# A linear-attention and channel-mix kernel: another written-out order, with a margin between VectorE's two-operand operations and GpSimd's, and k's exponentials placed without regard to k's maximum

## The chip, the cores and the metric

The kernel runs on one core of a Trainium2 chip. Its engines work side by side, each through its own queue in program order: TensorE (PE), VectorE (DVE), ScalarE (ACT), GpSimd (POOL) and SyncE (SP, which here only issues DMAs). The metric is the device time of one launch in microseconds. The time before is the median of three runs.

## The reference, cut to what matters

Two blocks, one after the other, for 8 batches of 576 positions:

- Attention, 8 heads of 64 wide: k and q are each projected by one 64 x 128 matrix; of every projected row the largest absolute value is subtracted (P - m), and phi is the concatenation of exp and exp of the negative of the shifted row, 256 features. Then kv = phi(k)^T v, z = the column sums of phi(k), and the output is phi(q) kv / (phi(q) z + 1e-6). There is no softmax over positions.
- Channel mix on the 576 x 512 result x: each row is mixed with the row before it, xk = mu_k x + (1 - mu_k) x_prev and likewise xr; then v = relu(xk Wk)^2 Wv with 1024 inner features, r = sigmoid(xr Wr), and the output is r v in float32.

## The kernel before, in words

**Tiling.** A batch has four *pairs* of heads; 32 pairs n = 4 b + a. Of a pair's positions eight chunks of 128 lie in "ps_k" and "ps_q", two PSUM banks each; the ninth part of every head, the *edge*, is handled for a whole batch at once (tp, rt, ekt, eqe and so on). The names of the steps of a pair, with their lines:

- kp, qp (PE, L570): the projections of k and q into PSUM. rk, rq (DVE, L583 and L588): the negated largest absolute value of each row, nmk and nmq.
- ea, eb (ACT, L609): exp of +ps_k and of -ps_k, 1024 columns each, read from the same PSUM tile that rk reads. The maximum isn't subtracted here; it enters through em (ACT, L595), which writes exp of +nmk and -nmk beside v, and va, vb (POOL or DVE, L601), which multiply v by it.
- kv (PE, L660), kc (copy to SBUF): the product with v. mh, mt, mc, qt (L619 to L640): q's projection once more, transposed and with its maximum added by a matmul; qa, qb (ACT, L647): its exponentials. nd (PE, L681): numerator and denominator; ra, rd (DVE, L689 and L693): the division, giving x.
- x is transposed by PE for pairs 0 to 7 (xt, xe, xf) and by a DMA that SP issues for the others (xz at L704, then xu, a shifted copy). df (L730): the difference of two neighbouring rows, DVE or POOL, two SBUF operands. xa and xb (DVE, L736): xk and xr from it, again two SBUF operands (SCALAR_TENSOR_TENSOR).
- For a batch: h (PE, L815, eight of four matmuls each), rl (relu: ACT L206 or DVE L208), sq (square: ACT, DVE or POOL, L212 and L214), r (PE, L834) and th (ACT, L840), v (PE, L848) and ob (DVE, L854), so (SP, L861: stores). he, rle, sqe, re, the, ve, obe, soe do the same for the edge of two batches.
- lk, lq (POOL, L324) and lv (POOL or SP, L330) load k, q and v; pt (PE, L341) transposes k and q of batches 0 and 1, pa and pb copy the result to qkT; for later batches SP issues a DMA transpose (tr, L355). lv goes into "vt", three buffers.

**PSUM** has three double tiles P0 to P2 and two single ones, M0 and M1; the number behind a colon in the order says which. "+9@0" asks for nine filling matmuls (L292) ahead of an operation.

**What sets the order.** The order of all 1498 operations is written out, in the string ORDER. A name may carry the engine behind a slash. The kernel runs through the list and issues each operation on its engine's queue; the list was made elsewhere by a planner, from the durations, dependences and "port" marks that the calls of op() still name. The kernel itself doesn't read these: op() keeps the function, the buffers and the choice of engine, and drops the rest, as these lines show. The semaphore waits are put in by the Tile framework, from what the instructions read and write, in program order.

```python
def op(self, name, eng, w, at, fn, deps=(), alloc=(), rel=(), chain=None, mode=0, port=False, alt=()):
    assert name not in self.ops, name
    self.ops[name] = dict(name=name, fn=fn, alloc=alloc, alt=alt, pe=mode if eng == "PE" else None)
```

Of the kernel before, what the change touches and what calls it, by code (L numbers as in the profile page):

```python
# [19 lines left out]
ident ones hk hq dve2 hk.d hq.d wphi wphi.d lk0.1 lk0.1.d lq0.1 lq0.1.d mus mus.d lk0.2 lk0.2.d dve3  # L20
lq0.2 lq0.2.d lv0.0/POOL lv0.0.d lk0.0.d/ACT lq0.0.d/DVE pt0.0:0+9@0 pt0.1:1 pa0/ACT pb0/DVE tr0
dve1 tp0.0:0+1@2 kp0:1 rt0.0 qp0:2 rk0 ekt0.0 mhe0.0/POOL lk1.0 lk1.0.d mte0.0:0+4@1 rq0 pt1.0:0 ea0
pt1.1:1 lq1.0 lq1.0.d pa1/ACT mce0.0/DVE pb1/DVE tr1 lv0.1/POOL lv0.1.d eb0 tp0.1:0+1@4 qp1:2
lv0.2/POOL lv0.2.d rt0.1 rq1 eme0.0 kp1:1+1@1 mh0/POOL ekt0.1 qte0.0:0 mhe0.1/POOL em0 rk1 eme0.1
eqe0.0 lk1.2 lk1.2.d mte0.1:2+3@1 pt2.0:1 mce0.1/ACT mt0:0 pt2.1:0 mh1/POOL pa2/DVE ea1 pb2/DVE tr2
va0/POOL pt3.0:1+1@4 mc0/DVE qp2:2 em1 pa3/DVE mt1:0 eb1 pt3.1:0 mc1/DVE vb0/POOL rq2 qt0:0 kp2:1
qa0 lq1.2 lq1.2.d pb3/DVE tr3 kv0:2 rk2 qb0 lk2.0 lk2.0.d pt4.0:0 mh2/POOL kc0/DVE ea2 pa4/DVE
va1/POOL mt2:0+2@1 qp3:2 mc2/DVE eb2 qt1:0 rq3 wk.0 wk.0.d qte0.1:0 pt4.1:1 eqe0.1 tp0.2:1 vb1/POOL
qa1 rt0.2 pt5.0:0 nd0:2 pb4/DVE tr4 ekt0.2 mhe0.2/POOL pa5/DVE pt5.1:1 ra0 qb1 rd0 lv1.0/POOL
lv1.0.d kp3:1 rk3 wk.1 wk.1.d wk.d eme0.2 kv1:2+1@0 em2 qp4:0 wr.0 wr.0.d kc1/ACT rq4 pb5/ACT tr5  # L30
mte0.2:2+1@0 xt0:0 wr.1 wr.1.d wr.d ea3 pt6.0:1 vb2/POOL mce0.2/DVE pa6/DVE qp5:0 eb3 qt2:2 rq5
qte0.2:1 mh3/POOL qa2 kp4:1 va2/POOL xe0/DVE mt3:0 xf0/DVE em3 mc3/DVE rk4 pt6.1:0 qb2 mh4/POOL
kv2:0 df0/POOL eqe0.2 kc2/DVE nd1:2 pb6/DVE tr6 ea4 nd2:0 lq2.0 lq2.0.d ra1 rd1 pt7.0:0 eb4 va3/POOL
pt7.1:1 ra2 pa7/DVE qt3:2 pb7/ACT tr7 rd2 mt4:1 xt1:0 vb3/POOL qa3 xf1/DVE xe1/DVE tp1.0:0 mc4/DVE
qb3 rt1.0 wv.0 wv.0.d kv3:1 kc3/ACT kp5:2 xa0 ekt1.0 xt2:0 nd3:1 rk5 mhe1.0/POOL xf2/ACT eme1.0
xe2/ACT df1/POOL ra3 ea5 rd3 xb1 eb5 xt3:0+7@1 mte1.0:1 qt4:0 xa1 xf3/ACT xe3/ACT qp6:2 xb0
mce1.0/ACT qa4 qt5:1+1@1 df2/DVE tr2.0 tr2.0.d tr8 tr9 qte1.0:0 df3/DVE qb4 xa2 em4 xa3 qp7:0+3@1
qa5 vb4/POOL rq6 h0.0:1+1@1 qb5 lv1.2/SP lv1.2.d va4/POOL rq7 tr2.2 tr2.2.d tr10 tr11 kp6:2
rl0.0/ACT kp7:1 eqe1.0 vb5/POOL rk6 kv4:0 sq0.0/ACT h0.1:1 kc4/ACT mh6/POOL rk7 ea6 va5/POOL nd4:0
eb6 h0.2:0 ra4 lk3.0 lk3.0.d rd4 rl0.1/ACT kv5:2 lv2.0/SP lv2.0.d xb3 rl0.2/ACT mt6:0 h0.3:1 kc5/ACT  # L40
xb2 mc6/ACT em6 ea7 sq0.1/DVE qp8:0 vb6/POOL nd5:2 rq8 eb7 r0.0:0 va6/POOL ra5 rl0.3/ACT rd5 tp2.0:1
th0.0 qt6:0 sq0.2/POOL rt2.0 qp9:2 qa6 h0.4:0 lq3.0 lq3.0.d rq9 qb6 r0.1:1 sq0.3/POOL ekt2.0
rl0.4/DVE qp10:0 qt7:2 wv.1 wv.1.d wv.d rq10 th0.1 kp8:1 vb7/POOL qa7 h0.5:0 rk8 mhe2.0/POOL qb7
kv6:0 rl0.5/DVE xt4:1 sq0.4/POOL kc6/ACT kp9:2 ea8 nd6:0 rk9 va7/POOL h0.6:0 eb8 tr3.0 tr3.0.d tr12
tr13 ra6 mh8/POOL rd6 eme2.0 qp11:1 sq0.5/POOL rl0.6/ACT rq11 kv7:0 em8 sq0.6/ACT vb8/POOL h0.7:0
ea9 kc7/DVE xf4/DVE xe4/DVE tr3.2 tr3.2.d tr14 tr15 mt8:0 nd7:1 va8/POOL mc8/ACT rl0.7/DVE eb9 qt8:0
ra7 rd7 va9/POOL qa8 mte2.0:2 xt5:0 mce2.0/DVE kv8:1 xe5/DVE vb9/POOL qb8 qte2.0:1 kc8/DVE kp10:2
xf5/DVE eqe2.0 qt9:1 rk10 df4/POOL lv2.2/SP lv2.2.d kp11:0 r0.2:0 lv3.0/SP lv3.0.d sq0.7/ACT rk11
mh10/POOL ea10 v0.0:1 lk4.0 lk4.0.d th0.2 df5/DVE qa9 xa4 v0.1:0 ob0.0 eb10 xa5 qb9 xb5 kv9:2 em10
xb4 tp3.0:1 ea11 v0.2:1 rt3.0 vb10/POOL kc9/ACT eb11 lq4.0 lq4.0.d ob0.1 nd8:2 ekt3.0 ob0.2  # L50
va10/POOL so0.1 so0.1.d nd9:0 ra8 rd8 mt10:1 xt6:1 vb11/POOL mc10/ACT xt7:0 eme3.0 ra9 xz8 xz8.d
qt10:1 xf6/ACT xe6/ACT rd9 kv10:2 va11/POOL qa10 xe7/DVE kp12:0 xz9 xz9.d kc10/DVE r0.3:1 rk12 qb10
df6/POOL kp13:2 so0.2 so0.2.d xf7/ACT th0.3 kv11:1 rk13 df7/POOL ea12 v0.3:0 kc11/DVE eb12 xa6 xa7
em12 qp12:1 ea13 qt11:0 rq12 va12/POOL h1.0:1 tr4.0 tr4.0.d tr16 tr17 eb13 mhe3.0/POOL ob0.3 qp13:1
rl1.0/ACT nd10:2 rq13 qa11 h1.1:1 qb11 xb6 h1.2:0 ra10 xb7 rl1.1/ACT mte3.0:0 nd11:1 mce3.0/ACT
# [105 lines left out]
def kernel(  # L161
# [58 lines left out]
    op = plan.op  # L220
# [5 lines left out]
    ident = consts.tile([128, 128], BF, name="ident")  # L226
# [813 lines left out]
```

## Time and profile before

| | |
|---|---|
| median of 3 runs | 277.08 us (276.7 to 278.89) |
| profiled execution | 277.05 us, its span 275.3 us |
| PE, DVE, ACT, POOL busy | 260.7, 229.5, 223.2, 157.8 us |
| largest groups | v on POOL 62 x 1205 ns; k and q exponentials on ACT 64 x 1042 each; maxima on DVE 32 x 1217 and 32 x 1216; xk and xr on DVE 64 x 836 |
| DMA | 42.89 MB, 156 GB/s on average |

The profile names instructions by line and by the tile written and read (out<-in). Its first part gives busy time per engine; the second cuts the span into 40 slices and gives the busy share of each in tenths; stretches of any length can be asked for as a table. A line of the waits reads: engine, tile and line that stood idle, what it waited for, the total in us, how often, the longest. A line of the time line gives the start, the duration, the engine, the line, the operation, and in square brackets the idle time before it with its releaser. An engine that isn't the bottleneck may idle at no cost.

### The profile page before, as it was taken

To read this page: it belongs to the slowest core of one execution; us is meant where nothing else is said; L and a number is where in the kernel's file an instruction comes from. 1 tells how busy PE (TensorE), PEld (TensorE's weight loads), DVE (VectorE), ACT (ScalarE), POOL (GpSimd) and SP (SyncE) were. 2 spreads that over 40 slices of the span, in tenths; PEclk is the share of its full clock that TensorE was granted. 3 is DMA by queue.
4 is the path that set the end of the run, shared out by engine and by line. 5 is a ranking of instruction groups with operands and counts; after the bars stand their busy time and mean duration, and the time that the engine had idled before them with its cause. 6 is when DMAs were issued, how large, how long until landed. Compare 5 with 4: busy or idle time off the path is not lost.

```text
span 275.3 us, 8896 instructions
## 1 busy us (share of the span) xinstructions
PE 260.7 (95%) x3692; PEld 153.8 (56%) x3736; DVE 229.5 (83%) x366; ACT 223.2 (81%) x410; POOL 157.8 (57%) x218
## 2 busy tenths in 40 slices
PE   7798999999999999999999899999999999999994
PEld 2465745565755655665565466565556654444552
DVE  5899999999999999999999799888849799834222
ACT  3699999999999999989989899999997855552430
POOL 5899827995858766596648863844565205111010
PEclk9999999999999999999999999999999999999999
DMA  7999999999997897979998899775244523504044
GB/s 152 217 234 231 205 189 196 204 147 241 203 185 139 200 219 165 206 209 182 197 187 166 130 194 208 176 229 64 64 116 100 63 62 66 133 5 116 2 114 114
DMA packets 65880, 42.89 MB, mean 156 GB/s; under 512 B 47152, under 2 KB 57008, under 8 KB 65840
## 3 DMA queue, kind: packets, MB, share of 16 engines
q1 hardware_dynamic: 54544, 27.77, 48.8%
q0 software_dynamic: 10992, 14.12, 29.6%
q8 instruction: 29, 0.48, 0.7%
q10 hardware_dynamic: 304, 0.43, 0.5%
q14 instruction: 11, 0.09, 0.1%
HBM read 33.62 MB, written 9.44 MB: 156 GB/s over the span
## 4 chain that ended last, share of the span: by engine, by line
PE 76%; ACT 9%; DVE 7%; issue 2%; DMA 2%; SPq 1%; POOL 1%; DVEq 0%; ACTq 0%; POOLq 0%
PE ps_v L848 19%; PE ps_h L815 17%; PE ps_r L834 10%; PE ps_nd L681 6%; PE ps_kv L660 5%; ACT q L647 4%; PE ps_qT L634 2%; PE ps_he L903 2%; PE ps_k L570 2%; ACT k L609 2%; PE ps_qT L640 2%; PE ps_q L570 2%; DMA vt<-in_v_dram 2%; PE ps_ve L935 2%; DVE nmk L583 2%
## 5 line engine op out<-in xcount | busy, mean ns | idle before, releaser
L601 POOL TENSOR_TENSOR v<-vt,v 128x576 bf16<-128x576 f32 x62 | 73.5, 1205 | 36.2 <-ACT v L595 33.5
L609 ACT ACTIVATE k<-ps_k 128x1024 bf16<-128x1024 f32 x64 | 64.0, 1042 | 1.3 <-DVE nmk L583 1.1
L647 ACT ACTIVATE q<-ps_qT 128x1024 bf16<-128x1024 f32 x64 | 63.0, 1042 | 2.2 <-PE ps_qT L640 2.0
L815 PE MATMUL ps_h<-xk,wk_bf 128*128 128x512 bf16 x239 | 62.3, 380 | 1.1 <-issue 0.2
L848 PE MATMUL ps_v<-wv_bf,kk 128*128 128x512 bf16 x240 | 58.2, 379 | 0.8 <-issue 0.2
L730 POOL TENSOR_TENSOR diff<-xs 128x576 bf16<-128x576 bf16 x21 | 28.1, 1347 | 30.9 <-DVE xr L736 19.1
L588 DVE TENSOR_REDUCE nmq<-ps_q 128x8 f32<-128x1024 f32 x32 | 38.7, 1216 | 1.1 <-PE ps_q L570 1.0
L848 PEld LDWEIGHTS <-kk 128*128 128x128 bf16 x256 | 23.8, 98 | 27.1 <-issue 0.2
L583 DVE TENSOR_REDUCE nmk<-ps_k 128x8 f32<-128x1024 f32 x32 | 38.5, 1217 | 0.5 <-PE ps_k L570 0.2
L854 DVE SCALAR_TENSOR_TENSOR ob<-rt,ps_v 128x512 f32<-128x512 bf16 x32 | 21.7, 684 | 18.0 <-PE ps_v L848 12.9
L815 PEld LDWEIGHTS <-wk_bf 128*128 128x128 bf16 x256 | 22.7, 98 | 24.7 <-issue 0.5
L206 ACT ACTIVATE krelu<-ps_h 128x512 bf16<-128x512 f32 x40 | 23.8, 607 | 15.2 <-PE ps_h L815 15.2
L834 PE MATMUL ps_r<-wr_bf,xr 128*128 128x512 bf16 x121 | 31.9, 380 | 0.4
L840 ACT ACTIVATE rt<-ps_r 128x512 bf16<-128x512 f32 x32 | 19.4, 608 | 14.7 <-PE ps_r L834 12.2
L214 POOL TENSOR_TENSOR kk<-krelu 128x512 bf16<-128x512 bf16 x17 | 17.8, 1047 | 18.2 <-ACT krelu L206 13.8
L693 DVE TENSOR_TENSOR x_sc<-ps_nd,rden 128x640 bf16<-128x640 f32 x32 | 26.0, 818 | 0.7
L736 DVE SCALAR_TENSOR_TENSOR xk<-diff,mu_k_t,xs 128x576 bf16<-128x576 bf16 x32 | 26.3, 836 | 0.1
L736 DVE SCALAR_TENSOR_TENSOR xr<-diff,mu_r_t,xs 128x576 bf16<-128x576 bf16 x32 | 26.3, 837 | 0.0
L660 PE MATMUL ps_kv<-v,k 64*128 64x65 bf16 x1024 | 22.7, 190 | 1.6 <-DVE x_sc L693 0.7
L208 DVE TENSOR_SCALAR krelu<-ps_h 128x512 bf16<-128x512 f32 x24 | 16.4, 683 | 8.8 <-PE ps_h L815 8.0
L660 PEld LDWEIGHTS <-k 64*128 64x128 bf16 x1024 | 19.7, 94 | 6.7 <-DVE nmq L588 1.5
L212 ACT ACTIVATE kk<-krelu 128x512 bf16<-128x512 bf16 x35 | 22.1, 641 | 1.3 <-DVE krelu L208 1.2
(105 smaller groups left out, 416.9 us busy)
## 6 DMA issues: line engine op xcount, KB each, us to landing
out_dram<-ob SPq DMA_DIRECT2D x70, 128.0 KB, 2.5
vt<-in_v_dram SPq DMA_DIRECT2D x12, 576.0 KB, 4.7
nat<-in_k_dram POOLq DMA_DIRECT2D x6, 576.0 KB, 6.8
nat<-in_q_dram POOLq DMA_DIRECT2D x6, 576.0 KB, 7.9
vt<-in_v_dram POOLq DMA_DIRECT2D x3, 576.0 KB, 6.7
wk_bf<-in_moe_w_k_dram POOLq DMA_DIRECT2D x2, 512.0 KB, 8.7
wv_bf<-in_moe_w_v_dram POOLq DMA_DIRECT2D x2, 512.0 KB, 8.5
nat<-in_k_dram POOLq DMA_DIRECT2D x3, 288.0 KB, 6.3
```

The source lines that it names most:

```text
L583: nc.vector.tensor_reduce(t[:, j, :], s["k"].rearrange("p a (g f) -> p (a g) f", f=128), axis=AX.X, op=ALU.max, apply_absolute_value=True, ...
L588: nc.vector.tensor_reduce(t[:, j, :], s["q"].rearrange("p a (g f) -> p (a g) f", f=128), axis=AX.X, op=ALU.max, apply_absolute_value=True, ...
L601: (nc.vector if eng == "DVE" else nc.gpsimd).tensor_tensor(vb[:, a, pn, :, 0:64], vt[b, a // 2][:, a % 2, :].rearrange("p (s d) -> p s d", ...
L609: nc.scalar.activation(s[f"k{pn}"], s["k"].rearrange("p a (g f) -> p (a g) f", f=128), AF.Exp, scale=(1.0 if pn == 0 else -1.0))
L647: nc.scalar.activation(t.rearrange("f x (a p) -> f x a p", a=2), s["qT"].rearrange("f a (x p) -> f x a p", p=64), AF.Exp, scale=(1.0 if pn ...
L660: nc.tensor.matmul(ps[:, hh, pn * 65:(pn + 1) * 65], lhsT=s[f"k{pn}"][r, c, :], rhs=vb[r, a, pn, 2 * g + par, :], start=(pn == 0 and c == ...
L693: nc.vector.tensor_tensor(s["x"].rearrange("p (b s) d -> p b s d", b=2), s["ndv"][:, :, :, 0:64], s["rd"].to_broadcast([128, 2, 5, 64]), o ...
L730: (nc.vector if eng == "DVE" else nc.gpsimd).tensor_tensor(s["d"], xs[:, a, 64:64 + S], xs[:, a, 0:S], op=ALU.subtract)
L736: nc.vector.scalar_tensor_tensor(out=t[:, a, (b % 2) * S:(b % 2 + 1) * S], in0=s["d"], scalar=mu[:, a:a + 1], in1=xs[:, a, 0:S], op0=ALU.m ...
L815: nc.tensor.matmul(ps, lhsT=wk_bf[:, c, fc * 128:(fc + 1) * 128], rhs=xkt[bp][:, c, m0:m0 + 512], start=(c == 0), stop=(c == NDC - 1))
L834: nc.tensor.matmul(ps, lhsT=xrt[bp][:, c, m0 + ci * 128:m0 + (ci + 1) * 128], rhs=wr_bf[:, c, :], start=(c == 0), stop=(c == NDC - 1))
L848: nc.tensor.matmul(ps, lhsT=s["kk"][:, fc, ci * 128:(ci + 1) * 128], rhs=wv_bf[:, fc, :], start=(fc == 0), stop=(fc == NFC - 1))
```

## The change

The string ORDER is replaced by another arrangement of the same 1498 operations, with other choices of engine and PSUM tile. In two calls of op() a named dependence is exchanged: ekt, the edge's exponentials of k, names tp instead of rt, and ea names kp instead of rk. In the new list the steps that have a choice of engine are spread so (before, then after):

| step | before | after |
|---|---|---|
| sq, sqe | ACT 39, DVE 13, POOL 20 | ACT 30, DVE 22, POOL 20 |
| rl, rle | ACT 47, DVE 25 | ACT 44, DVE 28 |
| df | DVE 11, POOL 21 | DVE 15, POOL 17 |
| va, vb | DVE 2, POOL 62 | DVE 3, POOL 61 |
| kc | ACT 17, DVE 15 | ACT 21, DVE 11 |
| mc, mce | ACT 16, DVE 12 | ACT 11, DVE 17 |
| xe, xf | ACT 7, DVE 9 | ACT 9, DVE 7 |
| xu | ACT 9, DVE 2, POOL 13 | ACT 10, DVE 3, POOL 11 |
| pa, pb | ACT 4, DVE 12 | ACT 2, DVE 14 |
| mhe | POOL 10 | POOL 9, DVE 1 |
| lv | POOL 5, SP 12 | SP 17 |
| filling matmuls | 36 | 28 |

The diff, cut to the ends of the list, the places of ea and rk of pairs 14, 21 and 24, and the two calls:

```diff
@@ -17,115 +17,114 @@
 ORDER = """
-ident ones hk hq dve2 hk.d hq.d wphi wphi.d lk0.1 lk0.1.d lq0.1 lq0.1.d mus mus.d lk0.2 lk0.2.d dve3
-lq0.2 lq0.2.d lv0.0/POOL lv0.0.d lk0.0.d/ACT lq0.0.d/DVE pt0.0:0+9@0 pt0.1:1 pa0/ACT pb0/DVE tr0
-dve1 tp0.0:0+1@2 kp0:1 rt0.0 qp0:2 rk0 ekt0.0 mhe0.0/POOL lk1.0 lk1.0.d mte0.0:0+4@1 rq0 pt1.0:0 ea0
-pt1.1:1 lq1.0 lq1.0.d pa1/ACT mce0.0/DVE pb1/DVE tr1 lv0.1/POOL lv0.1.d eb0 tp0.1:0+1@4 qp1:2
-lv0.2/POOL lv0.2.d rt0.1 rq1 eme0.0 kp1:1+1@1 mh0/POOL ekt0.1 qte0.0:0 mhe0.1/POOL em0 rk1 eme0.1
...
-so7.0.d so6.3 so6.3.d r7.3:0 ob7.1 he3.1:0 so7.1 so7.1.d th7.3 th7.2 v7.2:0 sqe3.0/ACT rle3.1/ACT
-sqe3.1/POOL v7.3:1 ob7.2 so7.2 so7.2.d re3:0 ob7.3 ve3.0:2 so7.3 so7.3.d the3 ve3.1:1 obe3.0
-soe3.0.b soe3.0.b.d soe3.0.a soe3.0.a.d obe3.1 soe3.1.a soe3.1.a.d soe3.1.b soe3.1.b.d
+ones ident hk hq dve2 hk.d hq.d wphi wphi.d lk0.1 lk0.1.d lq0.1 lq0.1.d lv0.0/SP lv0.0.d lk0.2
+lk0.2.d dve3 mus mus.d lq0.2 lq0.2.d lk1.0 lk1.0.d lk0.0.d/ACT lq1.0 lq1.0.d lq0.0.d/DVE lv0.1/SP
+lv0.1.d pt0.0:0+9@0 lk1.2 lk1.2.d pt0.1:1 pa0/ACT lv0.2/SP lv0.2.d pb0/DVE tr0 lq1.2 lq1.2.d dve1
+lv1.0/SP lv1.0.d tp0.0:0+1@2 kp0:1 rt0.0 qp0:2 rk0 eme0.0 mhe0.0/POOL ekt0.0 pt1.0:0+1@1 pt1.1:1
+wk.0 wk.0.d mte0.0:0 pa1/DVE mce0.0/ACT pb1/ACT tr1 rq0 wk.1 wk.1.d wk.d ea0 qp1:0+1@2 qte0.0:1 rq1
+kp1:2 mh0/POOL eb0 rk1 em0 mt0:0+3@0 tp0.1:1 eqe0.0 vb0/POOL pt2.0:0 mc0/ACT ekt0.1 pt2.1:1 pa2/DVE
...
+tr18 tr19 kc12/ACT kp14:2 qte3.0:1 sq1.2/POOL rq14 qp15:0 eqe3.0 r1.0:0 sq1.1/POOL rq15 ea14 nd11:1
+xu9/POOL h1.3:1 mh12/POOL th1.0 rk14 xu8/POOL vb13/POOL mt12:0 h1.4:0 rl1.3/ACT so0.1 so0.1.d ra11
...
+kp21:1 kc19/ACT qt20:0 ob2.1 ea21 qp23:2 lv5.2/SP lv5.2.d xa14 r2.3:0 eb21 rq23 df16/POOL v2.2:1
+qa20 rk21 xu17/POOL qb20 xu18/POOL df17/POOL nd19:2 th2.3 qt21:1 ra19 ob2.2 lk7.0 lk7.0.d h3.0:0
...
+he1.0:1 sq3.7/DVE tr7.0 tr7.0.d tr28 tr29 xb19 qb22 v3.0:0 xa19 qa23 rle1.0/DVE ea24 nd22:0
...
+r3.3:0 qb23 rk24 kv23:0 th3.3 xa18 kp25:1 kc23/ACT qt24:2 eme6.0 qp27:0 rle1.1/DVE df20/POOL qa24
...
+sq7.6/POOL th7.0 so6.2 so6.2.d r7.2:1 h7.7:0 he3.0:1 rl7.7/ACT th7.2 sq7.7/DVE he3.1:0 th7.1 v7.0:1
+rle3.1/ACT rle3.0/ACT sqe3.1/POOL v7.1:0 sqe3.0/DVE ob7.0 so7.0 so7.0.d r7.3:1 ob7.1 v7.2:2 so7.1
+so7.1.d th7.3 v7.3:0 ob7.2 so7.2 so7.2.d re3:2 ob7.3 ve3.0:1 so7.3 so7.3.d the3 ve3.1:2 obe3.0
+soe3.0.b soe3.0.b.d obe3.1 soe3.1.b soe3.1.b.d soe3.1.a soe3.1.a.d soe3.0.a soe3.0.a.d
 """
@@ -530,7 +529,7 @@
            alloc=[("mTe", ("mTe", tag))])
         op(f"eme{tag}", "ACT", 0.35, ("eme", it), eme, [f"rt{tag}"], rel=[("me", tag)],
            alloc=[("v1", ("v1", b))] if first else [], chain="eme")
-        op(f"ekt{tag}", "ACT", 0.4 + 0.21 * n, ("ekt", it), ekt, [f"rt{tag}"], rel=[A])
+        op(f"ekt{tag}", "ACT", 0.4 + 0.21 * n, ("ekt", it), ekt, [f"tp{tag}"], rel=[A])
         op(f"qte{tag}", "PE", 0.1 + 0.11 * n, ("qte", it), qte, [f"mce{tag}"],
            alloc=[("mo", ("mo", "q" + tag))], rel=[("mTe", tag), ("qkT", b)], mode=1)
         op(f"eqe{tag}", "ACT", 0.4 + 0.21 * n, ("eqe", it), eqe, [f"qte{tag}"], rel=[("mo", "q" + tag)])
@@ -754,7 +753,7 @@
             op("mc" + U, "DVE", 0.22, (K("mc"), n), mc, ["mt" + U], rel=[("P", "m" + U)], alloc=[("mT", ("mT", u))],
                chain="mc", alt=("DVE", "ACT"))
             op("em" + U, "ACT", 0.35, (K("em"), n), em, both("rk") + [f"eme{pt}"], rel=[("nmk", u)])
-        op("ea" + N, "ACT", 1.03, (K("ea"), n), ek(0), ["rk" + N], alloc=al("kpn"), rel=[("P", "k" + N)],
+        op("ea" + N, "ACT", 1.03, (K("ea"), n), ek(0), ["kp" + N], alloc=al("kpn"), rel=[("P", "k" + N)],
            chain="ea")
         op("eb" + N, "ACT", 1.03, (K("eb"), n), ek(1), ["ea" + N], rel=[("P", "k" + N)])
         for pn, vn in enumerate(("va", "vb")):
```

## The prediction

> **What bounds the kernel now.** I read the page first, its 40 slices, then the busy time by stretch, then who waited for whom.
>
> ```profile
> span 275.3 us, 8896 instructions
> PE 260.7 (95%) x3692; PEld 153.8 (56%) x3736; DVE 229.5 (83%) x366; ACT 223.2 (81%) x410; POOL 157.8 (57%) x218
> PE   7798999999999999999999899999999999999994
> DVE  5899999999999999999999799888849799834222
> ACT  3699999999999999989989899999997855552430
> POOL 5899827995858766596648863844565205111010
> ```
>
> PE is full from the third slice on; DVE and ACT are full too until about slice 22 and fall off towards the end, POOL never. The stretches say how much slack each has (the columns are length, then busy time and count for PE, weight loads, DVE, ACT, POOL):
>
> ```profile
> 20.00:40.20 20.20, 17.87 (x365) 12.76 (x365) 19.96 (x37) 19.22 (x40) 13.72 (x22) 1.00 1.14 204
> 40.20:60.00 19.80, 18.66 (x343) 10.94 (x345) 19.00 (x26) 19.70 (x36) 17.63 (x23) 1.00 1.17 197
> 60.00:80.00 20.00, 19.61 (x356) 12.38 (x360) 19.33 (x32) 19.27 (x35) 15.24 (x16) 1.00 1.11 200
> 80.00:112.50 32.50, 32.11 (x520) 19.93 (x523) 31.42 (x44) 30.57 (x56) 22.20 (x38) 1.00 0.94 184
> 139.00:169.50 30.50, 29.45 (x453) 17.79 (x454) 27.34 (x40) 28.69 (x54) 18.49 (x27) 1.00 0.90 172
> ```
>
> Three stages follow. Up to 40.2 us DVE leads (0.24 us idle in 20.2): ps_h can start only after the last xk of batch 0, which ends at 40.23; PE starts its first ps_h weight load at 40.25. From 40 to about 140, PE, DVE and ACT all run at 94 to 99%. After that PE alone is full. PE idles 14.6 us in all: 2.0 before 7.2, 4.5 up to 40.2, 1.5 up to 80, about 2.9 from there to its end at 271.6, and the last 3.7.
>
> The waits that concern the change:
>
> ```profile
> POOL v L601 <- ACT v L595: 33.5, 12, 7.3
> POOL diff L730 <- DVE xr L736: 19.1, 3, 12.7
> ACT k L609 <- DVE nmk L583: 1.1, 2, 0.7
> PE ps_e L469 <- DVE x_sc L693: 0.9, 2, 0.7
> ```
>
> POOL waits for data, not for its turn; ACT's wait for k's maximum is 1.1 us in all. The last line is where a DVE/POOL conflict does reach PE, at 153 us; here is the time line of it:
>
> ```profile
> 150.64 1.17 POOL L601 TENSOR_TENSOR v<-vt,v 128x576 bf16<-128x576 f32 x1 [0.86 <-ACT v L595]
> 150.65 1.77 DVE L736 SCALAR_TENSOR_TENSOR xk<-diff,mu_k_t,xs 128x576 bf16<-128x576 bf16 x1
> 152.59 0.82 DVE L693 TENSOR_TENSOR x_sc<-ps_nd,rden 128x640 bf16<-128x640 f32 x1
> 153.47 0.40 PE L469 MATMUL ps_e<-wph,qkT 64*128 64x128 bf16 x8 [0.73 <-DVE x_sc L693]
> ```
>
> An xk that usually takes 0.81 (its median) took 1.77 beside a POOL v begun 10 ns earlier; x_sc came late and PE sat still for 0.73 us.
>
> **What the Trainium skill says.** SBUF — State Buffer, "Who interferes with whom": a VectorE instruction with two SBUF inputs and a GpSimd instruction that reads SBUF exclude each other, whichever starts second waits. The lines above agree in kind: the xk lost 0.96 us, a little less than the 1.17 of the v beside it. PSUM — Partial Sum Buffer, "PSUM bank collisions raise a hardware error": no two of TensorE, ScalarE and VectorE may touch one bank in the same partitions at once, reads against reads included. The trace fits software that keeps them apart: in all 32 pairs the first exponential of k starts after the maximum ended, 0.03 us after it for pairs 0 and 1, where ACT stood idle. DMA: Bandwidth & Descriptors, "Issuing engines are not separate DMA queues": transfers share 16 engines whoever issues them, so moving loads to SP buys issue time only. No run here tests the sharing; the page's DMA row stands at 7 to 9 tenths for the first 130 us.
>
> **The change, part by part.** Only the list is read by the kernel; the dependences named in op() are not used when it is built. So the two edited lines change nothing by themselves, and the effect is that of the new list. I counted both lists with the durations of this trace (an instruction's own; for one that changes engine, the median of its kind on the new one).
>
> 1. *k's exponentials.* Both still read the same PSUM tile as the maximum, so the semaphore wait stays, by program order. In 29 of 32 pairs the maximum still precedes; for 14, 21 and 24 it follows, and will wait for ACT instead, which by then is done. Upper bound of the gain: ACT's 1.1 us. The list's words between maximum and exponential fall from 11.8 to 8.4 on average; converted by the PE work between them, only pairs 0, 4, 26 and 30 come closer than the 1.25 us that the maximum takes, by 0.05 to 0.35 us. Behind a waiting exponential on ACT lie krelu and rt, for which PE's two M banks wait. Value +0.3, bounds -1.1 and +2.
>
> 2. *The margin.* v (62 at 1205 ns against 1155 undisturbed) loses 3.1 us to conflicts in sum, xk and xr (64 at 836 against 810) 1.7, of which the case above is 0.96 and one at 231.96 (1.83 long) is 1.02, without a PE wait after it. POOL's share is covered by its 43% idle time. On the path there is one PE stall of 0.73. Value -0.7, bounds -1.7 and 0.
>
> 3. *Work that changes engine.* DVE gets 7 more squares and 2 more of the edge (9 x 0.42), 4 more diff (0.45), 3 more krelu (0.69), 3 mce, 2 mc (0.21), 2 copies of qkT (0.44), 1 v (0.72), 1 xu and 1 mhe, and gives away 4 kv copies (0.42) and 2 xe: +8 us. ACT loses 7, POOL 11. Up to the first ps_h DVE has 61 instructions before and 60 after, with 0.2 us less; ACT, up to pair 5's exponentials of q, 0.1 less. So the first stage keeps its work. From there to the first ps_h of batch 2 (112.5 us) DVE's list grows by 1.2 us while PE's shrinks by 0.6: 1.8 us net, against 2.55 us that DVE idled between 40.2 and 112.5. To batch 5's first ps_h it is 9.4 against 4.2 more PE work: 5.2 net, against 8.9 idle. It fits, but more than half the slack goes, and what is late next is the evacuation of PSUM by DVE. Value +1.0, bounds 0 and +4.
>
> 4. *Loads.* Five v loads go from POOL's queue to SP's. Four of them (1728 KB, batch 0 and the first half of batch 1) are issued there within the first 6 us or so, since no buffer holds them back: there are three vt, all free. They used to stand behind lk and lq: the last at 21.3. The trace's landings: lq0.1 7.5, lq0.2 10.6, lv0.0 (288 KB) 0.7 us later, lq1.0 14.6. At 0.7 us per 288 KB the four are 4.3 us of the DMA engines' time, all of it pulled in front of 17 us; if the queues share, between half and all of it lies ahead of lq0.2, which then lands at 12.7 to 14.9. PE's transposes of pair 2 wait for that, with everything behind them on PE, and DVE's copies of them, with the maxima behind those. Before, these copies began at 13.34; the new list has 0.6 us less on DVE ahead of them, so DVE would be ready at about 12.8. They begin 0.4 after the landing: 13.1 to 15.3, that is -0.2 to +2.0 against before. This delay stays: DVE leads this stage, and has no slack in it. The eight nat loads that POOL now issues in a row (0.75 each, 1.4 to about 7.4) end before mhe0.0, which ran at 7.70. Value +1.2, bounds -0.5 and +3. On SP, the transposes of x (1.23 to issue, 3.7 to land) are placed on average 8.6 instead of 10.9 us ahead of their use, at the least 3.5 (pair 31): hidden while other PE work remains, 0 to +1, taken as 0.
>
> 5. *Fill matmuls.* 28 instead of 36, each 0.213: -1.7 if PE had work instead, 0 where it would wait anyway. The first nine are the same in both; nearly all others stand in the DVE-led stage. Value 0.
>
> 6. *PE's order.* Changes between 64-row and 128-row matmuls number 120 in both lists, and the real matmuls are the same: nothing.
>
> 7. *The end.* One of the last stores on SP now waits behind the other, after both halves are done; an issue there takes 0.47, and the last landing ends the span. Value +0.4.
>
> Sum: 0.3 - 0.7 + 1.0 + 1.2 + 0.4 = +2.2. The profiled execution took 277.05 (span 275.30 and 1.75 around it), the median of the runs is 277.08; so 279.3.
>
> **Rivals.** *Much slower: DVE becomes the bound of the middle (chance 0.20).* By pair 15's second projection of k the new list has 4.9 us more DVE work since the first ps_h and only 2.4 more PE work. If DVE can't use its last 2.5 us of idle time, krelu and the maxima hold M and P banks longer and PE stops; it never makes this up, as it has no slack to 271. Each stage then costs its net: 2.5, and again 1.8 between batches 3 and 5 (half of 5.2 - 1.7): +4.3 in place of the 1.0, so 282.6. It decides once DVE is busier than about 98% between 40 and 112 us. Against it: 96 to 97% there before, with hardly a PE wait. *Faster (0.16).* If the loads do no harm and PE and DVE lose 3 us less at the start (fills 1.7, DVE's 0.4 at each of two edge maxima, 0.5 at the copies) and the conflicts go (-0.7): 273.4. It decides at lq0.2: landed before 12.4, DVE never waits. Against it: DVE idles only 0.24 us from 20 to 40 us, and its work there is the same. *The edited ties do nothing and the new order is worth the old (0.20).* Without terms 1, 3 and 4: 276.8.
>
> **How the numbers follow.** Runs spread by 0.8% (276.7 to 278.9), so about 1% (2.8 us) is what a measurement can tell. The forecast has 0.44: its own range is 277 to 282, and about half of it lies over 279.85. Slower by over 1%: 0.20 + 0.23 = 0.43; within 1%: 0.20 + 0.21 = 0.41; faster 0.16. The range for 8 in 10 goes down to 274.0 (just short of the full gain) and up to 283.5 (the DVE rival and a little of the loads' upper bound).
>
> **What would show it.** Right: PE's transposes of pair 2 wait for a DMA until 13 us or later; first ps_h at 41 to 42.5; xk and xr with a mean near 810 and no 1.8; v near 1165; an exponential of k never before its maximum has ended where it follows in the list; DVE 97 to 98% from 40 to 112. Wrong: first ps_h before 40 (faster), or PE idle above 2 us between 80 and 140 with DVE as releaser (much slower).

## The result

The changed kernel takes 289.75 us (median of 4 runs, 287.62 to 291.81) against 277.41 for the kernel before, run beside it: a ratio of 1.044, with an interval of 1.034 to 1.054. The forecast was 279.3, with 274.0 to 283.5 around it. The profiled execution took 291.06 (span 289.3 and 1.76 around it), so the span grew by 14.0 us. Ratios here and below leave out runs more than 1.5% above the fastest of their kernel; medians are of all runs, and the profiled executions of e5, e11, e12 and e18 are among those left out.

The first lines of the page of the changed kernel answer to those shown of before (DMA is the busy share of the DMA engines in tenths, GB/s what they moved):

```profile
span 289.3 us, 8873 instructions
...
PE 260.4 (90%) x3684; PEld 153.6 (53%) x3730; DVE 235.8 (82%) x388; ACT 218.2 (75%) x399; POOL 144.9 (50%) x202
...
PE   6879889997079999999989999999999999999993
...
DVE  6999999998048999899989989998988689763132
ACT  3899999998048899989798999989989463442520
...
PEclk9999999999559999999999999999999999999999
DMA  7999998999990989699999989983723405323334
GB/s 171 202 286 211 211 210 171 190 229 180 98 142 16 169 192 245 125 132 286 209 137 183 160 127 149 205 248 70 118 58 122 97 2 118 79 57 73 75 73 110
```

PE is as busy in sum as before (260.4 against 260.7), DVE has 6.3 us more. But the eleventh and twelfth slices, from 72 to 87 us, hold a hole in which PE, DVE and ACT stop together, and TensorE's clock falls to half in it. The same by stretch (columns as in the table of before; the seventh figure is the granted clock, the last GB/s):

```profile
40.00:60.00 20.00, 18.54 (x358) 11.49 (x362) 19.83 (x30) 19.70 (x34) 18.47 (x23) 1.00 1.01 184
60.00:70.00 10.00, 9.74 (x189) 6.38 (x189) 9.93 (x19) 10.00 (x18) 5.04 (x6) 1.00 1.16 234
70.00:82.00 12.00, 1.25 (x17) 0.61 (x17) 1.13 (x2) 1.28 (x3) 5.40 (x7) 0.64 1.34 120
82.00:90.00 8.00, 7.84 (x114) 3.89 (x110) 5.98 (x8) 5.31 (x10) 0.81 (x1) 0.69 0.61 100
```

Between 70 and 82 PE worked 1.25 us. Between 82 and 90 it was busy again, at 0.69 of its clock: 8 x 0.31, by my estimate some 2.5 us of work lost once more. In that hole the chain of what ended last (start, length, what) has a single piece, and the waits (total, times, longest) name the same one:

```profile
60.20 0.53 SPq L329
...
60.83 0.41 SPq L329
...
61.29 20.24 DMA qkT<-nat
...
81.58 0.40 PE ps_e L468 x4
```

```profile
DVE mT L201 <- PE ps_m L995: 10.9, 1, 10.9
...
PE ps_e L468 <- DMA qkT<-nat: 10.7, 1, 10.7
```

PE waited 10.7 us for the DMA transpose tr3.2 (k and q of pairs 14 and 15), from 70.8 to 81.6 us; tp3.0 (the edge projection of batch 3, ps_e) reads what it writes. Before, tr3.2 was issued at 61.79 and landed at 67.73, 5.9 us later. Now it was issued at 61.29 and landed 20.24 us later. SP's line of before (start, length of the issue), then SP's and GpSimd's own lines of the changed kernel show what was issued with it:

```profile
61.79 2.71 SPq L355 DMA_TRANSPOSE qkT<-nat  x1
```

```profile
60.20 1.04 SPq L329 DMA_DIRECT2D vt<-in_v_dram  x2
61.29 8.96 SPq L354 DMA_TRANSPOSE qkT<-nat  x1
```

```profile
61.24 0.81 POOL L323 DMA_DIRECT2D nat<-in_k_dram  x1
62.05 0.75 POOL L323 DMA_DIRECT2D nat<-in_q_dram  x1
```

Two v loads (lv2.2, lv3.0) stand directly ahead of it on SP; a load of k and one of q (lk4.0, lq4.0) leave GpSimd 0.05 us before and 0.76 us after its issue began, and land 15.2 and 19.1 us later. Before, all four left later than tr3.2: the v loads at 64.6 and 65.2, lk4.0 at 65.4, lq4.0 at 71.0. The issue alone held SP for 8.96 us (2.71 before). A smaller hole follows at 146 us: 1.2 us at nd18, behind a transpose of x that landed 12.4 us after its issue among bulk loads of batches 4 to 6.

Up to the hole the changed kernel was ahead: first weight load for ps_h at 39.46 us (40.25 before), for ps_v at 63.13 (65.00).

### The profile page after: what moved, and what is told of

The parts are those of the page before. It is cut to its first block, busy times and chain, and to the rows that moved or that the text cites. A ratio compares the mean times of both kernels' runs of the same rounds, so it can differ in the third digit from the quotient of the medians.

```text
span 289.3 us, 8873 instructions
## 1 busy us (share of the span) xinstructions
PE 260.4 (90%) x3684; PEld 153.6 (53%) x3730; DVE 235.8 (82%) x388; ACT 218.2 (75%) x399; POOL 144.9 (50%) x202
## 4 chain that ended last, share of the span: by engine, by line
PE 68%; DMA 14%; DVE 12%; ACT 2%; issue 1%; SPq 0%; DVEq 0%
PE ps_v L847 17%; PE ps_h L814 17%; DMA qkT<-nat 9%; PE ps_r L833 8%; PE ps_nd L680 5%; PE ps_kv L659 5%; DMA xs<-x_sc 4%; DVE nmq L587 4%; PE ps_ve L934 2%; PE ps_he L902 2%; PE ps_q L569 2%; DVE nmk L582 2%; PE ps_qT L633 2%; DVE xk L735 2%; PE ps_k L569 2%; PE ps_qT L639 2%
## 5 line engine op out<-in xcount | busy, mean ns | idle before, releaser
L600 POOL TENSOR_TENSOR v<-vt,v 128x576 bf16<-128x576 f32 x61 | 70.4, 1174 | 49.3 <-ACT v L594 43.2
L608 ACT ACTIVATE k<-ps_k 128x1024 bf16<-128x1024 f32 x64 | 63.3, 1030 | 0.9 <-DVE nmk L582 0.5
L814 PE MATMUL ps_h<-xk,wk_bf 128*128 128x512 bf16 x240 | 61.4, 380 | 1.3 <-issue 0.6
L847 PE MATMUL ps_v<-wv_bf,kk 128*128 128x512 bf16 x244 | 59.9, 387 | 1.1 <-issue 0.3
L729 POOL TENSOR_TENSOR diff<-xs 128x576 bf16<-128x576 bf16 x17 | 22.1, 1302 | 28.4 <-ACT xs L709 8.7
L213 POOL TENSOR_TENSOR kk<-krelu 128x512 bf16<-128x512 bf16 x18 | 19.1, 1066 | 32.6 <-ACT krelu L205 28.0
L205 ACT ACTIVATE krelu<-ps_h 128x512 bf16<-128x512 f32 x39 | 23.1, 603 | 14.9 <-PE ps_h L814 14.3
L833 PE MATMUL ps_r<-wr_bf,xr 128*128 128x512 bf16 x116 | 31.1, 379 | 0.9 <-issue 0.5
L569 PEld LDWEIGHTS <-qkT 64*128 64x128 bf16 x512 | 16.8, 95 | 9.5 <-issue 7.7
L680 PE MATMUL ps_nd<-kv,q 128*128 128x65 bf16 x512 | 21.4, 193 | 0.0
```

What stands on the lines that cost most here:

```text
L569: nc.tensor.matmul(ps[:, par, g * 128:(g + 1) * 128], lhsT=qkT[b][r, g0 + gg + g, :], rhs=wph[r, :], start=(g == 0), stop=(g == 3))
L600: (nc.vector if eng == "DVE" else nc.gpsimd).tensor_tensor(vb[:, a, pn, :, 0:64], vt[b, a // 2][:, a % 2, :].rearrange("p (s d) -> p s d", ...
L608: nc.scalar.activation(s[f"k{pn}"], s["k"].rearrange("p a (g f) -> p (a g) f", f=128), AF.Exp, scale=(1.0 if pn == 0 else -1.0))
L680: nc.tensor.matmul(ps[:, bk, o * 65:(o + 1) * 65], lhsT=tail if sl < 2 else s[f"q{pn}"][:, 2 * G + h, :], rhs=s["kv"][:, h, pn, :], start= ...
L814: nc.tensor.matmul(ps, lhsT=wk_bf[:, c, fc * 128:(fc + 1) * 128], rhs=xkt[bp][:, c, m0:m0 + 512], start=(c == 0), stop=(c == NDC - 1))
L833: nc.tensor.matmul(ps, lhsT=xrt[bp][:, c, m0 + ci * 128:m0 + (ci + 1) * 128], rhs=wr_bf[:, c, :], start=(c == 0), stop=(c == NDC - 1))
```

## The experiments

Two theories stood at the start. **J**: a jam of transfers delays tr3.2, and the rest of the change is worth little; either the v loads ahead are at fault (J-v), or the loads of k and q at the same time (J-kq), or it takes both together (J-both). **D**: VectorE's greater load and the new order cost the time by themselves. All edits are to the list of words; "after" is the changed list, "before" the old one. "lk4.0" stands for the word and its landing word together.

### Moving the four loads round tr3.2

```diff
e1  after:   - lv2.2/SP - lv3.0/SP (ahead of tr3.2)       + both behind tr15 (behind tr3.2)
e2  after:   - lk4.0 - lq4.0 (at tr3.2)                    + lk4.0 ahead of vb10, lq4.0 ahead of va10
e3  after:   e1 and e2 together
e4  before:  - lv2.2, lv3.0, lk4.0, lq4.0 (behind tr3.2)   + all four directly ahead of tr3.2
```

> The changed order, with only the two v loads on SP (lv2.2, lv3.0; 576 KB each) moved behind the DMA transpose tr3.2. Theory J-v (the two v loads queued ahead of tr3.2 are what holds it): tr3.2 lands within 8 us of its issue, the gap of 10.7 us before tp3.0 shrinks below 2 us, the time is 276 to 280 us. Theory J-kq (the loads of k and q, issued by GpSimd while tr3.2 is being issued, hold it): tr3.2 still lands 15 us or more after its issue, the gap stays above 7 us, the time is 286 us or more. Theory D (VectorE's 10 us more of work and the new order cost the time by themselves; the gap only sits where the loss shows): the gap may go, the time stays above 285 us.

> The changed order, with only the loads of k and q of batch 4 on GpSimd moved: lk4.0 from ahead of va8 to just ahead of vb10, lq4.0 to just ahead of va10. Theory J-kq: tr3.2 lands within 9 us of its issue, the gap before tp3.0 shrinks below 2 us, 276 to 280 us. Theory J-v: tr3.2 lands 15 us or more after its issue, 286 us or more. If both pairs of loads are needed for the jam (J-both), this and the run with the v loads moved each get most of it back: gap of 0 to 5 us, 277 to 284 us. Theory D: above 285 us.

> The changed order with both moves: lv2.2 and lv3.0 behind tr3.2, lk4.0 and lq4.0 ahead of vb10 and va10. Every theory of the jam: no gap above 2 us before tp3.0, TensorE's clock stays at full speed there, tr3.2 lands about 6 us after its issue; 10.7 us of gap and about 2 us of halved clock gone, so 276 to 278.5 us, level with the kernel before. Theory D: 285 us or more.

> The kernel before, with its four loads lv2.2, lv3.0, lk4.0 and lq4.0 moved ahead of tr3.2 as the changed order has them; nothing else is touched. Theories of the jam: tr3.2 lands 15 to 20 us after its issue, TensorE stands 6 to 12 us before tp3.0 and its clock is halved for some us after it: 285 to 291 us. Theory D: the kernel before keeps its time, 276 to 279 us.

Beside a kernel before of 277.85: e1 285.93 (ratio 1.024, 1.014 to 1.033), e2 290.23 (1.040, 1.031 to 1.049), e3 282.54 (1.013, 1.004 to 1.022), e4 285.28 (1.024, 1.016 to 1.031). So the kernel before, with nothing but four loads moved, gets the hole and is 7.4 us slower; its waits show

```profile
PE ps_e L469 <- DMA qkT<-nat: 6.4, 1, 6.4
```

That speaks for J. But none of the three repairs gave the whole back, and D's number for e1 came true for another reason. On tr3.2 itself e1 fits neither J-v (within 8 us) nor J-kq (15 or more). In e1 and e3 the hole at tp3.0 is gone (tr3.2 landed 9.6 and 8.1 us after its issue), and a new wait took its place. From e3, between 71 and 75 us:

```profile
POOL v L600 <- DMA vt<-in_v_dram: 8.8, 1, 8.8
...
PE ps_m L995 <- POOL mhl L619: 2.5, 1, 2.5
```

GpSimd, which works its queue in order, stood 8.8 us at vb10 for lv2.2, now behind tr3.2 and slowed by lk4.0; mh10, queued behind vb10, came late, and PE with it. In e2 the load of k was issued at 62.9 instead of 61.2, still only 0.5 us behind tr3.2 (62.4): GpSimd had run idle and reached the moved word at once. Tr3.2 landed 19.0 us after its issue. Beside e1, where lk4.0 left 0.9 us behind it and it landed after 9.6, this says that the v loads ahead count once a load of k is there.

### Which loads hold the transpose

```diff
e5  after:   - lk4.0 - lq4.0 (at tr3.2)   + lk4.0 ahead of va10, lq4.0 behind va10 (both behind vb10)
e6  after:   e5 and e1 together
e7  after:   e6, and - lv5.0 (behind lv4.2)   + lv5.0 ahead of tr6.0
e8  before:  - lk4.0 - lq4.0   + both directly ahead of tr3.2 (the v loads stay behind)
```

> The changed order with the v loads where the change put them (ahead of tr3.2) and the loads of k and q of batch 4 moved further than before, to both sides of va10, so that GpSimd issues them at about 70 us, after vb10, some 8 us behind the issue of tr3.2 instead of 0.5. Theory J-kq (what holds tr3.2 is a load of k or q running at the same time): tr3.2 lands within 8 us of its issue, the gap before tp3.0 is below 1 us, 276 to 280 us. Theory J-v (v loads ahead are enough): tr3.2 lands 12 us or more after its issue, the gap stays above 4 us, 284 us or more.

> As the run before, and the two v loads behind tr3.2 too. With all four loads behind it, tr3.2 lands within 7 us, and lv2.2, with no load of k ahead of it, lands within 5.5 us of its issue (8.0 with lk4.0 ahead of it), so that the wait of GpSimd for it, which became 2.55 us of TensorE's, goes: 279 to 281 us. What is then left against the kernel before is the smaller jam near 130 us (1.2 us of TensorE) and the rest of the change. Theory J-v expects this run to be 4 us or more below the run with the v loads ahead; theory J-kq the two within 1.5 us of each other.

> The run before, with lv5.0 also moved, from right behind lv4.2 to just ahead of tr6.0, so that near 120 us one v load less stands ahead of xz15. If the second jam (transposes xz issued behind lk6.0, lv4.2 and lv5.0 land 12 us later) costs what its gap shows: xz15 lands within 9 us, the gap of 1.2 us before nd18 is gone, 1 to 1.5 us less than the run before. If the gap was slack that a later wait takes: no difference (below 0.4 us).

> The kernel before with only the loads of k and q of batch 4 (lk4.0, lq4.0) moved ahead of tr3.2; its v loads stay behind. Theory J-kq: tr3.2 lands 10 us or more after its issue, a gap of 3 us or more before tp3.0, 281 us or more. Theory J-v: tr3.2 within 8 us, 277 to 279.5 us.

Beside 277.68: e5 284.54 (1.024, 1.018 to 1.030), e6 285.06 (1.021, 1.010 to 1.031), e7 288.80 (1.042, 1.036 to 1.047), e8 283.37 (1.020, 1.014 to 1.027). On tr3.2 the answer is clear when four runs of the changed list are put side by side. Its time to landing, with neither pair of loads near it (e6), with the two v loads alone ahead (e5; lk4.0 and lq4.0 leave at 71.6 and 73.6), with k and q alone (e1), and with both (the change):

```profile
DMA to landing us min/median/max: 4.8/4.8/4.8
...
DMA to landing us min/median/max: 8.6/8.6/8.6
...
DMA to landing us min/median/max: 9.6/9.6/9.6
...
DMA to landing us min/median/max: 20.2/20.2/20.2
```

Alone each pair of loads adds 3.8 to 4.9 us, and PE does not wait for tr3.2; together they add 15.5. So it is J-both in this order. Two things differ a little between these runs: the v loads that aren't ahead follow 3 us behind tr3.2, and lk4.0 leaves 0.04 us ahead of it in the change and 0.9 behind it in e1. But e2, with the v loads ahead, lk4.0 0.5 us behind and lq4.0 9 us behind, still gives 19.0. In the order before, the loads of k and q by themselves do more: in e8 they leave 1.5 and 0.7 us ahead of tr3.2, which lands after 11.2 us, and PE stands 2.6 us at tp3.0; with the v loads too (e4) it lands after 13.0, and PE stands 6.4.

All transposes of qkT in the sixteen profiles with whole loads (before, after, e1 to e12, e15, e16), 192 in number, sorted by the loads on their way near them. A load counts if it was issued no later than 2.5 us after the transpose's own issue and had not landed 0.5 us after it. Loads of k and q and of weights go through GpSimd, those of v nearly all through SP; the numbers are read from the issue and landing times in the traces, and the sorting was made after the runs:

| on their way near it | transposes | landing after issue, us: least, median, most | over 9 us |
|---|---|---|---|
| none | 97 | 4.5, 5.3, 7.1 | 0 |
| v only | 35 | 4.5, 7.5, 8.6 | 0 |
| k, q or weights only | 48 | 4.6, 6.6, 16.5 | 5 |
| both | 12 | 10.1, 13.4, 20.2 | 12 |

The twelve are few different cases: tr6.2 six times, tr3.2 five times, tr2.2 once. With a limit of 3 us instead of 2.5 a thirteenth joins them, tr3.2 of e3, which landed after 8.1.

The prediction of the times, though, failed again: e5 and e6 are not at 280, and e7, which should have won 1 us, lost 4. E6 has new waits of PE where the moved loads of k and q now run: 2.1 us at ps_kv for a v that GpSimd reached late, 1.3 us for a transpose of batch 4, 2.5 us for one of batch 5. And e5 and e7 show a second mechanism (in e5 in the profiled execution of 292.74 us; its other three took 282.85 to 285.33). In e7, first GpSimd, then DVE:

```profile
147.87 0.81 POOL L323 DMA_DIRECT2D nat<-in_k_dram  x1
148.70 4.54 POOL L600 TENSOR_TENSOR v<-vt,v 128x576 bf16<-128x576 f32 x4
```

```profile
147.96 5.89 DVE L735 SCALAR_TENSOR_TENSOR xk<-diff,mu_k_t,xs 128x576 bf16<-128x576 bf16 x1 [1.40 <-POOL diff L729]
153.78 0.81 DVE L692 TENSOR_TENSOR x_sc<-ps_nd,rden 128x640 bf16<-128x640 f32 x1
154.64 0.61 PE L569 MATMUL ps_k<-wph,qkT 64*128 64x128 bf16 x8 [5.17 <-DVE x_sc L692]
```

An xk of usually 0.81 us, begun 0.09 us into GpSimd's issue of lk7.0, took 5.89 us: it ended 0.6 us behind the row of four v that followed on GpSimd without a pause. x_sc stood behind it on DVE, and PE stood 5.2 us. The same happened in e5 (5.90 us, PE 5.2) and in e10 below (5.44 us, PE 4.3). In 16 other cases, over the profiles of all runs but the next, an xk or xr also began during an issue of GpSimd's, but the next operation there followed 0.35 us or more after the issue; it took 0.80 to 0.82 us each time. The last run takes the issue out from ahead of that row:

```diff
e18  e7:  - lk7.0 (ahead of va20 vb20 va21 vb21)   + lk7.0 behind vb21
```

> The run with lv5.0 moved too (tr3.2 first, k and q loads behind va10, lv5.0 ahead of tr6.0), with one more load moved: lk7.0 from ahead of GpSimd's row of four v (va20, vb20, va21, vb21) to behind it. There xk (pair 18's) took 5.89 us and TensorE stood 5.2 us. Theory S (an xk that begins during GpSimd's load issue, with v operations directly behind it, is held until the whole row is done): without the load there, the xk takes at most 2 us, the gap of 5.2 us goes, 281.5 to 284.5 us. Theory R (the row of v by itself holds it): the xk still takes 4.5 us or more, the gap stays, 286 us or more. Either way tr6.2, which had begun together with lk7.0 and took 14.3 us to land, is expected to land within 9 us.

Beside 277.60, 282.51 (1.013, 1.005 to 1.022). In its profile the gap is gone, no xk or xr took over 1.8 us, and tr6.2, which had begun together with lk7.0 and landed 14.3 us later, landed after 6.4. It is the number of theory S; but in this run the row of v began 1.2 us after the xk ahead of it, so the row by itself was not tried, and R stays open. An operation directly behind the issue isn't enough by itself: in e18 an xr began 0.47 us into the issue of lk7.0, with two small operations of GpSimd (0.52 and 0.22 us) right behind, and took 0.81 us.

### The loads' places in the list, and the start

```diff
e9   after:   every load of k, q, v and transpose of qkT of batches 2 to 7 put where before has it, counted in TensorE's words (lv6.0 also on its engine of before)
e10  before:  the same ones put where after has them (lv6.0 on after's engine)
e11  after:   only the loads of k and q put where before has them
e12  before:  - the loads of batches 0 and 1, lk2.0, lq2.0   + at after's places, v on SP
```

> The changed order, with every bulk load of k, q and v and every DMA transpose of qkT of batches 2 to 7 put back to the place, counted in TensorE's words, that it has in the kernel before; all compute words, ties, engines and the start stay as changed. Theory L (the places of the loads hold the whole loss, everything else in the change is worth about nothing): 275.5 to 279.5 us, no gap of TensorE above 1.3 us after 20 us, every transpose of qkT landed within 9 us. Theory D (VectorE's load, the ties or the margin cost something too): 282 us or more without any such gap.

> The mirror: the kernel before, with the same loads and transposes of batches 2 to 7 at the places, counted in TensorE's words, that the change gives them. Theory L: 285 to 291 us, with transposes of qkT that land 12 us or more after issue and gaps of TensorE of 8 us or more in sum behind them. Theory D: 277 to 280 us.

> The changed order, with only GpSimd's loads of k and q of batches 2 to 7 put back to their places of before; v loads and transposes stay where the change puts them. Theory J-kq (a transpose is slow when a load of k or q runs at the same time, whatever the v loads do): all transposes of qkT land within 10 us, 276 to 280 us, within 1.5 us of the run with everything put back. Theory J-v: 283 us or more.

> The kernel before, with the loads of batches 0 and 1 (and lk2.0, lq2.0) at the change's places and engines: v loads on SP from the start, the loads of batch 1 ahead of the weights. The prediction's step 4 priced the new start at +1.2 us: 278 to 279.5 us. The profile after says the opposite (v0.0 of the first batch started 1.9 us earlier): if the loads are the cause of that lead and it is kept to the end, 275 to 276.5 us; if the lead is due to the order of the compute, 277 to 278 us.

Beside 277.50: e9 293.19 (1.056, 1.050 to 1.063), e10 294.22 (1.060, 1.057 to 1.064), e11 293.16 (1.046, 1.039 to 1.053), e12 285.66 (1.009, 1.005 to 1.013). E10 went as L expected and past it: tr3.2 landed after 13.9 us, PE stood 5.7 us at tp3.0 and 4.3 behind the xk named above. E9 and E11 fell: back at their old places, the loads did not go back to their old times. In e11 lk4.0 and lq4.0 left at 62.4 and 63.2, tr3.2 at 61.75 landed after 19.7 us, and the 10.7 us are there again. A place in one common list fixes only the order on the issuing engine. In before, GpSimd had df4 and mh10 ahead of lk4.0 and got there at 65.4; in the new order that work is done earlier or elsewhere, and GpSimd issues the load as soon as it is free. In e9 tr3.2 did land (6.7 us), but PE waited elsewhere: 2.8 us behind GpSimd's queue at 74 us and 2.2 at 178, 3.3 behind DVE at 107, and 1.5 for a transpose of qkT at 185; that is 9.8 us in sum, less than the 15.7 by which it is slower; the rest is not placed. E12 came out above all three of its forecasts. In its profiled execution of 289.15 us, tr2.0 began 0.03 us before a load of weights and landed after 16.5 us, tr2.2 after 19.4, and PE stood 7.6 us. The ratio of 1.009 rests on two runs of 280.0 us that left no trace, so what cost them 2.5 us is not shown.

### The rest of the change by itself

```diff
e13, e14  before, after:
-  in_=heads(src, b, a0, a1)         (k, q; likewise v)
+  in_=heads(src, b, a0, a1)[0:16]   for batches 2 to 7, into 16 of the 128 partitions; nat and vt as fixed tiles (shortened)
```

These kernels leave out seven eighths of those loads; the rest of each buffer keeps old data, so the output is not the reference's. The operations and their order stay.

> The kernel before with its loads of k, q and v of batches 2 to 7 cut to 16 of 128 partitions (an eighth of the bytes; same number of instructions, same places, same waits; the rest of each buffer keeps old data, so the output is not the reference's). The buffers are fixed tiles instead of rotated ones. It shows what this order takes when bulk loads crowd nothing. Theory L and theory D: 275 to 277.5 us, since the kernel before has no gap behind a load above 0.8 us.

> The changed order with the loads cut in the same way. Theory L (places of the loads hold the whole loss, and the rest of the change is worth about nothing): within 1.5 us of the run of the kernel before with its loads cut, transposes of qkT landed within 7 us, no gap of TensorE above 1 us after 20 us. If the earlier start of the changed order (1.9 us ahead at the first v0.0) is kept, it is 1 to 3 us faster than that run. Theory D: 3 us or more slower than that run, without such gaps.

Beside 277.38: e13 277.71 (1.000, 0.998 to 1.002), e14 276.72 (0.995, 0.993 to 0.998). This settles D: with an eighth of the load bytes of batches 2 to 7, the changed order is 1.0 us faster than the order before, not 12 slower. The kernel before has nothing to win from lighter loads; the changed one wins 13.0 us. The profile of e14 has no hole, and full clock where it was:

```profile
PE   6798898999999999999999999999999999999993
...
PEclk9899999999999999999999999999999999999998
```

### Staggered loads

```diff
e15  after:  - lv3.0/SP (ahead of tr3.2)   + behind tr15 (lv2.2 stays ahead)
             - df5/DVE   + df5/POOL
             - lk4.0, lq4.0 (at tr3.2)     + lk4.0 ahead of vb10, lq4.0 ahead of va10
e16  e15:    - lv4.2 (ahead of xz15)   + behind it;   - lv5.0   + ahead of tr6.0
```

> The changed order with the loads around tr3.2 staggered: lv2.2 stays ahead of it, lv3.0 goes behind it, df5 goes from VectorE to GpSimd and lk4.0 behind that (ahead of vb10), lq4.0 ahead of va10. lk4.0 is then issued about 2.5 us behind tr3.2 instead of 0.5 ahead. Theory L: tr3.2 lands within 8 us, the gap before tp3.0 and the 2.55 us wait for lv2.2 both go: 278 to 280.5 us. Theory D: 282 us or more.

> The run before, with the second jam opened as well: lv4.2 moved from ahead of xz15 to behind it, lv5.0 to just ahead of tr6.0. xz15 then lands within 8 us instead of 12.5 and the 1.2 us gap at nd18 goes: 1 to 1.5 us less than the run before, 276.5 to 279.5 us, unless a later transpose collides with lk7.0 as one did when only lv5.0 was moved (then 284 us or more).

E15 282.43 (1.012, 1.000 to 1.023), above L's forecast, e16 278.37 (1.000, 0.997 to 1.004), beside the same 277.38. In e16 lk4.0 leaves at 64.6, 3.1 us behind tr3.2, which lands after 8.5 us with PE not waiting; xz15 lands after 6.2 us (12.6 in e15). Five loads and one diff moved, and the changed kernel is level with before. It beats it by nothing that can be told; e14 says that at most some 0.7 us were to be had.

### k's exponentials

Of the freed pairs, only 14, 21 and 24 use their freedom in the new list. With e14 as the base:

```diff
e17  e14:  - rk14, rk21, rk24 (behind ea14, ea21, ea24)   + each directly ahead of its ea
```

> The changed order with the loads of batches 2 to 7 cut to an eighth (output not the reference's), and in the three pairs where the change lets k's exponential go ahead of k's maximum (14, 21, 24) the maximum put ahead again, so that no pair uses the freedom. The prediction's step 1 says that the untied pairs bring nothing, since both read the same tile of PSUM and one waits for the other anyway: the same as the run with cut loads within 0.5 us (276.2 to 277.2 us). If the freedom is what makes the changed order faster, 277.5 us or more, level with the kernel before with cut loads.

Beside 277.41, 280.64 (1.010, 1.007 to 1.013): 3.9 us slower than e14. I had expected nothing. The waits of three short stretches (85 to 92, 140 to 147 and 166 to 171 us) each hold one such line:

```profile
ACT k L612 <- DVE nmk L586: 2.0, 1, 2.0
PE ps_h L818 <- ACT rt L843: 1.9, 1, 1.9
...
ACT k L612 <- DVE nmk L586: 1.7, 1, 1.7
...
ACT k L612 <- DVE nmk L586: 1.2, 1, 1.2
```

ACT stood 4.9 us in three waits for a maximum that DVE, full as it is here, reached late; rt, or q's exponentials, stood behind on ACT, and PE waited for them with 1.9, 1.2 and 0.5 us. In e14 this wait is 0.3 us in sum. The run shows what the freedom is worth in this order; an order made with the tie would have placed other words there.

## Why the prediction was wrong

**Where it failed: step 4.** It priced the loads of the start, and of the transposes on SP only those of x: "hidden while other PE work remains, 0 to +1, taken as 0". The transposes of qkT, which stand on the same queue, and the loads of batches 2 to 7 were not looked at; in the sum they stand at nothing. They are the whole loss: +13.3, the 12.3 between the two kernels and the 1.0 by which the changed one is ahead once the loads are light. (For the transposes of x alone the 0 was nearly right: the trace shows 1.2 us, at nd18.) The list showed the thing needed: lv2.2 and lv3.0 ahead of tr3.2 instead of behind, lk4.0 and lq4.0 five and seven words behind it instead of 36 and 57.

In the trace of before tr3.2 lands after 5.9 us, but that is not a property of the instruction: it holds while no load is on its way near it. The Trainium skill, DMA: Bandwidth & Descriptors, "Queues, rings and completion order", says that each DMA engine takes turns, packet by packet, between the queues that have work for it. A sharing of that kind would slow a transpose that has loads beside it, and the medians of the table rise so: 5.3 us with none, 13.4 with a load of v and one of k, q or weights. That the sharing is what slows the transpose is argued, not shown, and why the two kinds together cost more than both apart stays open. The page TensorE: Matmul & The Clock Gate, "Part 1: The HAM clock gate", has the clock halved after about 3.4 us of idleness. The trace agrees in kind, with a shorter time: the clock fell to half at 73.3 us, 2.5 us after PE's last matmul, and was full again at 87.0, 5.4 us after PE had work again. This put some 2.5 us (the estimate above) on top of the 10.7.

**The start in step 4** had the wrong size. lq0.2 landed at 11.62 us, not at 12.7 to 14.9, and the first ps_h came at 39.46, not at 41 or later (39.5 to 41.2 over all profiles of the changed order). By its own sign (lq0.2 before 12.4) the rival "faster" was met here; but of its 3 us the trace shows 0.8 at the first ps_h and 1.9 at the first ps_v, and with light loads 1.0 is left at the end. In the order before, the new start cost 0.9% (e12); whether by the first stage or by the transposes of batch 2 is not shown.

**Step 1** had the wait right and its worth wrong. An exponential never begins before its maximum's end where it follows (0.03 us behind it for pairs 1, 16 and 25), and ACT's waits fell from 1.1 to 0.5 us in sum. But the 1.1 us, read in the order before, was taken as the bound of the gain: in the new order, where DVE is fuller, the three pairs that go first are worth 3.9 us.

**Step 2** is right in part: v fell from 1205 to 1174 ns, xr from 837 to 809; but xk rose from 836 to 849, since three of them take 0.96 to 1.52 us. What I left out is the conflict that did not stand in the trace of before, an xk of 5.4 to 5.9 us beside a GpSimd issue with a row of v's behind it. The shift of some loads by a few us was enough to bring it about, in both orders. **Step 3**: DVE was busy 99% from 40 to 60 us, more than the 97 to 98 given, and this held nobody up; with light loads 235.4 us of DVE go with 276.7 us in all. The rival "DVE becomes the bound" named the place (PE idle above 2 us from 80 to 140) nearly, with the wrong releaser. **Step 7**: from PE's last matmul to the end it is 4.3 us instead of 3.7: +0.7 for +0.4.

In sum, steps 1, 2, 3, 5, 6 and 7 with the start stood at +2.2; with light loads they measure -1.0 (e14 less e13). That is nearest to the rival that had the ties do nothing, but by luck: in this order the freedom, which that rival put at nothing, is worth 3.9 us (e17). How the rest divides among margin, fills and start was not tried.

## What to carry to other kernels

The landing time of a DMA transpose read from a trace is that of its neighbours too: when a change moves loads, list for each transpose what is issued within some 3 us of it or still on its way, on every queue, and price the collision before anything else, above all where two kinds of load meet (here up to 15 us on one transpose). A word's place in a common list is no time: follow the issuing engine's own queue, since taking work off it makes its loads leave earlier. And where an order is tight, measure its compute apart from its transfers by cutting the bytes: e13 and e14 answered what moving loads in the twelve runs before them had not, whether the order itself costs time.

## What the runs showed of the hardware

- One transpose of qkT (two pairs) lands 4.5 us after its issue at best and 20.2 at worst; its issue holds SP for 2.4 to 10.8 us, so that all behind it on SP leaves late as well. It landed after more than 10 us whenever a load of v and one of k, q or weights were both on their way near it, counted as in the table (12 of 12), and never after more than 8.6 with v alone (35).
- A load of k or q suffers likewise: 15.2 and 19.1 us beside tr3.2, 7.9 and 8.9 in the trace of before. The bytes fall: the eleventh slice of the changed kernel, with the DMA engines 90% busy or more, moved 98 GB/s, the ten slices before it 171 to 286.
- An xk on VectorE that began during GpSimd's issue of a load (0.81 us), with a row of v operations directly behind it, took 5.4 to 5.9 us, three times out of three; with 0.35 us or more of pause behind the issue, 0.80 to 0.82 us in 16 of 16. Whether the row alone would do the same was not tried.
